# Clustered attention with a gated convolution on one core: two row moves become one transfer, an earlier load of the convolution weights, and another order

## The chip, the cores and the metric

The kernel runs on one core of a Trainium2 chip. The metric is device time in microseconds (us) of one execution. The median of three executions of the kernel before is 464.64 us (461.85 to 464.67). The engines are TensorE (PE in the rows; its weight loads PEld), VectorE (DVE), ScalarE (ACT), GpSimd (POOL) and SyncE (SP), which here issues every transfer between memories.

## The reference

Four batches of eight heads, 768 positions, 64 channels a head; then a gated projection over the 512 channels of a batch.

```python
q_assign = argmax(q_n @ c_n, axis=-1); k_assign = argmax(k_n @ c_n, axis=-1)
mask = q_assign[:, :, :, None] == k_assign[:, :, None, :]
scores = where(mask, scale * q @ k.T, -1e9)
attn = exp(scores - max(scores)); attn = attn / (sum(attn) + 1e-9)
x = (attn @ v)                       # heads side by side: [B, S, 512]
gate = sigmoid(causal_conv5(x, conv_w))
out = (gate * (x @ w_val)) @ w_out
```

The mask depends on the argmax over 16 clusters, so q and k are split into a high and a low part and their products are added up, to keep more digits than one pass of the product gives.

## The kernel before

There are 32 heads, taken in pairs (16 pairs, `p` below); four pairs make a batch. For a head `h` the work is:

- **Operands.** `load_both` (L438) loads kT and qT into alternate partitions of one `raw` tile. `prep_hi` (XH) rounds it to the high part in `ops[h][0]`, on ScalarE or VectorE (L217 or L219), and `prep_lo` (XL) makes the low part on VectorE (L213). Then transfers within the core's memory (`move`, L451) deal the rows out: MA copies the odd rows of the high part (q's) to the even rows of operand 2, MB copies the same rows to the even rows of operand 3, MC copies q's low part to the odd rows of operand 2, and MD overwrites the odd rows of operand 0 with its even rows, so MD has to wait until MA and MB have read. MK (`prep_mask`, L588) puts the cluster rows into operands 1 and 3.
- **Products.** QK (L624, L629) makes a tile of 128 x 768 scores from the four operands; six tiles a head. EX (L652) is their exponential on ScalarE, AD (L213, tile `ad`) adds the six tiles of a head together on VectorE.
- **Sums and values.** When a pair's adds are done, LL (L695) sums over partitions on TensorE; AV (L769) multiplies the probabilities with v (tile `vt`). SX (L785) scales the result on VectorE, five PC0/PC steps (L219 or L217, L800) are the convolution, PX and PL split it into high and low parts.
- **Projections.** "val" (L844) is x times w_val, VO (L850) applies the gate, VH and VL split the result, "proj" (L875) is its product with w_out. TensorE has 3 products for each step of 128 channels of either.
- **Clusters.** SI (L502) takes the similarities of a pair with the centroids; AM, A1, A2, A3 and FM make the cluster rows from it.

Every engine takes its instructions in a fixed order. For most of the program that order is written out as the table `PLAN`: 630 operations of VectorE, 681 of TensorE and those of the others, each number one operation of the list `todo`, with V or A for the engine where both can do it. The start stands ahead of it in code, and there the order is that of the lines: `load_cen`, `load_first`, `load_head(1, ...)`, `load_conv` (the convolution weights, 20 KB, tile `cbuf`), `load_v(0)`, `load_both(2)` and `load_both(3)`. CW (`prep_conv`) decodes these weights on VectorE with eight small instructions; PC of pair 0 needs them.

Of the kernel before, what the change touches and what calls it, by code (L numbers as in the profile page):

```python
# [8 lines left out]
F32 = mybir.dt.float32  # L9
# [8 lines left out]
P = 128  # L18
# [136 lines left out]
def kernel(  # L155
# [266 lines left out]
    raws, vs, ops, cleared = {}, {}, {}, {}  # L422
# [548 lines left out]
    for h in range(2, NH):  # L971
        if h < 4:
            LT = held("raw")
        else:
            LT = dma("LT", load_both, h, take="raw", after=[LT])
        LTS[h] = LT
        war = [last_qk[h - 2]] if h > 2 else []
        XH = Op("XH", "AV", prep_hi, h, after=[LT] + war)
        XL = Op("XL", "V", prep_lo, h, after=[XH]).frees(LT)
        z = [ZM[h]] if h in ZM else []  # L980
        MA = dma("MA", move, h, 2, 0, 0, 1, after=[XH])
        MB = dma("MB", move, h, 3, 0, 0, 1, after=[XH] + z)
# [3 lines left out]
        low[h], ready[h] = [MC, *z], [XL, MA, MB, MC, MD]  # L986

# [80 lines left out]
    for b in range(B):  # L1068
# [54 lines left out]
        591V 583 576 0 594 799.0 577 1 801A 800A 578 589A 579 2.0 580 581 587V 585A 3 1492 1415 w10.2 802.2 588A 4.1  # L1123
        603 610 6 586A 7.2 1416A 592 w11.0 9 12 10 11.3 803 13.4 582 584A 804 997.0 998 15 999 16.5 805 1417 1418
        1001A 1000A 593 806 14.0 5.1 1419 17 814.2 18 19.6 21 807.0 808 1420 596 815 1421 816 22.7 1002.1 1003.3 809
        1404 24 25.8 27 1422 28.9 29 8 1004 595 810 811 30 982 33 20 31.10 597A 34.11 599 590A 598 1005 1006 817 1007
        600 36 39 1008 1405A 37 601 1009 38.0 32 813 818 23 40.3 1423A 42 602 819.0 1406 45 1010 43.12 46.13 35 812
        1424 820 48 49.14 51 52.15 26 1014.2 1407 1408 1015 617 1425 624 54 1437 1409 41.0 604A 55 56.1 57 58.4 605
        1011 44 1410 47 1012 60 821 63 1016 61.2 64.5 1022.0 606 608 1017 1023 50 59.1 607 823 1024 1025A 826.2 1438A
        66 1018 1026A 822 827 69 611A 53 609 1019 612 614 613 67.6 70.9 615 1013 1027.0 1028.2 1029 1411 631 638 62 72  # L1130
        75 73 1412A 825 616 1439 65 1030 828 74.7 1031 1020 1021 78 68 824 1413 71 829 76.10 81 79.8 82.11 1414 1032
        983 830 84 85.0 87 1039.1 838.3 88.1 90 1040 831.1 1440 1041 618A 77.0 832 93 1033 1441 91 619 1442 1047.1
        1042 621 620 92.3 1048 94.4 622 96 99 833 97.2 100.12 95.1 1034 102 103.5 80 1443 1043 835 83 1049 98 1426 834
        105 623 839 1044 1035 1050A 625A 1051A 628 101 627 1493A 626 629 1036 837 1037 1038 86 1444 1052.1 106.13 108
        109 1427A 1495A 645 630 110.6 111 112.14 840 1053.3 1054 114 104 836 1445A 117 115.9 1045 1046 107 118.15 89
        841 1501A 1428 1055 120 121.3 984 1446 1429 123 124.7 1064.0 1065 126 652 1496 842 632A 1066 635 127 1430
        128.4 633 634 129 1056 1057 1497 636 1447 130.10 1067 843.2 844 1498 845 637 131.0 132 133.2 135 1072.0 1073
        136.8 1068 1499 850.2 1431 138 141 851 1494 847 134 639A 1058 1074 1059 846 1432 1060 1061 1062 1076A 139.11
        1503A 1069 142.12 1075A 849 642 659 641 113.1 144 147 145 146.0 148.5 116 1063 137 640 1077.0 150 153 1433 985
        1078.2 1079 1070 1080 1081 852 119 1082 140 154.1 122 151.13 643 143 1434A 1083 125 1504 1435 156 666 157.4  # L1140
        644 159 853 1436 1089.1 160.6 848 162 163 1090 1071 165 1505 854 1084 1085 646A 1091 649 1448 164.10 1097.1
        166.14 1098 648 168 1092 171 862.3 1500 169.2 172.9 1099 1506 647 1093 174 177 1100A 855.1 650 1101A 1094 651
        1449A 856 1502 1507 857 149.0 863 858 1450 167.1 152 1451 653A 656 864 1509A 1086 1087 1088 1102.1 1103.3 1104
        1105 986 654 859 1106 1107 1452 865 155 861 1510 1096 657 178.8 1108 1109 1095 655 175.15 1110 1508 170 673
        680 1525A 1111 1517A 1112 1113 658 180 1533.2 183 866 867.0 181 173 1518 1511A 860 182.3 1534 176 184.11 158
        186 187.7 189 179 868 1535 161 192 190.12 1536 193.0 195 198 1453 869 660A 1537 1454 1114.0 196.10 662 199
        874.2 663 661 1115 1455 664 875 200.5 871 1526 201 202.14 1456A 1586.0 185.0 1457 204 1116 876 207 205.13
        208.1 1122.2 1123 1124 1126A 203.1 877 1519A 1587 1588 1589 1590 210 211.2 213 1579.2 665 214.9 667A 1117 1580
        1512 870 216 1118 1458 1125A 219 1540.0 1541 1542 217 1581 220.15 218.4 668 1513 1514 222 669 1515 206 223.8
        1543 1544 225 226.6 1459 1582 1583 1527A 1460A 188 1119 1121 1461 228 670 1520 231 1127.0 1128.2 1462 873 1129  # L1150
        1463 674A 1464 1130 1131 1132 1133 229.3 987 687 878 1516 677 1134 1135 1465 1466 671 872 675 1136 1137 1138
        1467A 232.5 879.3 1468 1120 1469 1593.1 672 678 880 881 191 676 209 1470 194 212 234 237 235 236.11 1594 215
        197 883 694 1595 1596 1547.3 1548 240 1549 1471A 238.14 882 1597 1472 1139.1 241.7 1473 1140 243 244.13 1550
        1474 1475 1476 1147.1 679 1141 1477 1478A 1148 1551 246 247.12 1479 1480 1149 1481 249 1554.1 250.1 681A 1528
        252 253 254.0 683 1600.3 1142 1601 1602 1150A 255 256.2 258 1521 1603 684 261 1529 1522 1555 1530 1531 1556
        1557 682 1523 1151A 259.9 1482A 262.10 1143 1524 1483 885 1484 1485 1558 1532 1604 1625A 1486 1487 1488 264
        267 688A 1152.1 1489A 1153.3 1154 1155 1156 685 1157 1144 239.0 1490 988 1491 1146 1158 265.11 1159 691 1145
        1538A 884 1559V 686 1545A 886.2 1539 268.14 1560 1552A 221.1 270 1553 273 1546 701 708 271 272.4 224 1567.0
        887 888 274.15 689 1568 1569 1570 1172.2 1571 276 1173 227 277.8 279 1573.0 280.6 1174 692 889 890 690 693
        1633A 1572 1574 1575 891.2 242 230 892 282 1576 893 1176A 1175A 1561.2 1562 1563 1564 285 1577 283.7 245 248  # L1160
        1565 286.13 251 898.0 233 1584V 1585 1164.2 1626 895 894 288 291 1627A 715 899 1578 1165 695A 1605A 1160 1566
        1628 1166 1629 697 1161 897 289 698 290.3 1162 292.12 1630 1167 1163 294 1598A 297 1631 1632 696 1177.0 1178.2
        1179 1180 1181 1182 1183 1184 275.0 257.1 260 278 263 281 284 1168 1185 1186 1187 1188 298.1 266 989 295.5 300
        303 699 1169 1171 1170 722 269 287 910.3 301.4 702A 304.0 900 1189.1 901 902 1591A 896 700 306 309 911 704 307
        1592 703 1190 1191 706 1599 1606 903.1 1635V 1636 1192 308.2 310.15 1607.3 1608 904 905 311.0 705 312 315 1609
        1610 313.8 907 906 316.9 1634 318 321 1611 322.10 1619.1 1620 912 913 1197.3 1198 319.6 1637 314 1199 1621
        1622 707 324 325 327 914 1193 709A 710 1638 1639 1201A 326.7 328.11 1613.3 1614 1200A 317 330 909 320 333 1194
        1195 1651V 711 1615 1612 712 1623 293.1 915.1 331.14 334.13 1616 1649V 336 339 323 916 1650 296 716A 1624
# [173 lines left out]
```

## Time and profile before

| what | value |
|---|---|
| median of 3 executions | 464.64 us (461.85 to 464.67) |
| profiled execution | 463.09 us |
| its span, first to last instruction | 461.4 us |
| TensorE busy | 448.8 us (97%) |
| VectorE busy | 409.6 us (89%) |
| ScalarE busy | 296.0 us (64%) |
| GpSimd busy | 7.5 us (2%) |
| mean granted TensorE clock | 0.997 of full speed |
| transfers, mean | 137 GB/s |

The profiled execution is 1.55 us under the median and 1.69 us longer than its span. A busy share counts an instruction from its start to its end; TensorE's products overlap, so that its busy time is no measure of its work: the distance from one start to the next is. The chain of waits goes back from the last instruction, at each step to what released it.

### The profile page before, as it was taken

The page shows a single profiled execution, that of the slowest core. Times are in us where ns is not written, and L with a number is a line of the kernel's source. Part 1 is how long each engine was busy: PE and PEld are TensorE (multiplying, and loading weights), DVE is VectorE, ACT ScalarE, POOL GpSimd, SP SyncE. Part 2 cuts the span into 40 slices and gives each one's busy share as a digit, 9 for nine tenths or more (in the row PEclk, how much of TensorE's full clock was granted, in tenths as well). Part 3 has the DMA queues.
Part 4 walks back from the last instruction along what each step waited for, and adds up shares of the span by engine and source line. Part 5 has one row for each costly group of instructions (what it writes and reads, how often), then busy time and mean ns, then how long its engine had stood idle before and what let it go on. Part 6 is the DMA issues. An engine that isn't in the chain of part 4 may idle for free.

```text
span 461.4 us, 7538 instructions
## 1 busy us (share of the span) xinstructions
PE 448.8 (97%) x2633; PEld 320.1 (69%) x2633; DVE 409.6 (89%) x725; ACT 296.0 (64%) x437; POOL 7.5 (2%) x47
## 2 busy tenths in 40 slices
PE   7899999999999999999999999999999999999995
PEld 5556555654794968558597784948677696848984
DVE  4999999999999999999999998989998788796950
ACT  6988789867885787738584664768854465613131
POOL 5000000000000000000000000000000000001000
PEclk9999999999999999999999999999999999999998
DMA  7546656446446453544543156335542313200112
GB/s 213 196 141 209 203 167 223 169 139 200 143 131 198 146 185 123 167 119 138 172 150 133 53 186 213 102 131 170 184 160 83 105 46 100 82 0 25 45 38 105
DMA packets 32775, 63.38 MB, mean 137 GB/s; under 512 B 10588, under 2 KB 12764, under 8 KB 32732
## 3 DMA queue, kind: packets, MB, share of 16 engines
q1 hardware_dynamic: 32732, 62.85, 42.1%
q8 instruction: 22, 0.36, 0.3%
q14 instruction: 21, 0.17, 0.1%
HBM read 29.81 MB, written 6.38 MB: 78 GB/s over the span
## 4 chain that ended last, share of the span: by engine, by line
PE 72%; DVE 12%; DMA 8%; ACT 3%; SPq 2%; issue 2%; DVEq 0%; ACTq 0%
PE acc L769 20%; PE sp L624 12%; PE acc L875 11%; PE acc L844 11%; PE sp L629 10%; DVE ad L213 4%; DMA op<-op 2%; PE acc L695 2%; PE sp L844 2%; PE sp L875 2%; DVE gate L800 2%; PE acc L502 2%; ACT pt L652 1%; SPq L588 1%; DVE op L213 1%
## 5 line engine op out<-in xcount | busy, mean ns | idle before, releaser
L652 ACT ACTIVATE pt<-sp,sp 128x768 f32<-128x768 f32 x192 | 166.2, 898 | 58.6 <-PE sp L629 26.8
L769 PE MATMUL acc<-pt,vt 128*64 128x384 f32 x768 | 131.1, 490 | 0.6 <-ACT vt L217 0.6
L213 DVE TENSOR_TENSOR ad<-ad,pt 128x768 f32<-128x768 f32 x128 | 119.4, 951 | 2.0
L624 PE MATMUL sp<-op,op 128*128 128x384 f32 x372 | 101.9, 355 | 3.3 <-ACT pt L652 1.7
L769 PEld LDWEIGHTS acc<-pt,vt 128*64 128x64 f32 x768 | 52.2, 137 | 67.9 <-issue 61.7
L629 PE MATMUL sp<-op,op 128*128 128x384 f32 (+1 forms) x372 | 95.5, 337 | 0.0
L624 PEld LDWEIGHTS sp<-op,op 128*128 128x128 f32 x372 | 62.7, 188 | 30.0 <-ACT pt L652 15.8
L800 DVE SCALAR_TENSOR_TENSOR gate<-xr,cw,gate 128x768 f32<-128x768 f32 (+1 forms) x84 | 68.5, 823 | 0.9
L629 PEld LDWEIGHTS sp<-op,op 128*128 128x128 f32 (+1 forms) x372 | 67.4, 188 | 0.0
L875 PE MATMUL acc<-wh_o,h 128*128 128x512 f32 x144 | 51.3, 399 | 0.0
L844 PE MATMUL acc<-xh,wh_v 128*128 128x384 f32 x112 | 38.6, 344 | 0.0
L844 PE MATMUL acc<-xh,wl_v 128*128 128x384 f32 x112 | 37.8, 337 | 0.0
L844 PE MATMUL acc<-xl,wh_v 128*128 128x384 f32 x112 | 37.7, 337 | 0.0
L875 PEld LDWEIGHTS acc<-wh_o,h 128*128 128x128 f32 x144 | 27.1, 188 | 5.7 <-issue 0.6
L213 DVE TENSOR_TENSOR ad<-pt,pt 128x768 f32<-128x768 f32 x32 | 30.2, 948 | 0.8 <-ACT pt L652 0.8
L213 DVE TENSOR_TENSOR op<-raw,op 128x768 fp32r<-128x768 f32 (+2 forms) x34 | 30.4, 902 | 0.1
L875 PE MATMUL acc<-wl_o,h 128*128 128x512 f32 x72 | 28.6, 397 | 0.0
L881 ACT ACTIVATE ob<-acc 128x512 f32<-128x512 f32 (+1 forms) x22 | 12.5, 575 | 19.6 <-PE acc L875 16.5
L850 DVE SCALAR_TENSOR_TENSOR gate<-gate,acc 128x384 f32<-128x384 f32 x28 | 15.1, 549 | 8.5 <-PE acc L844 7.6
L217 ACT ACTIVATE op<-raw 128x768 fp32r<-128x768 f32 x24 | 20.2, 840 | 1.8 <-PE sp L624 1.8
L844 PEld LDWEIGHTS acc<-xh,wh_v 128*128 128x128 f32 x112 | 21.1, 188 | 0.2
L844 PEld LDWEIGHTS acc<-xh,wl_v 128*128 128x128 f32 x112 | 21.1, 188 | 0.2
(174 smaller groups left out, 483.8 us busy)
## 6 DMA issues: line engine op xcount, KB each, us to landing
op<-op SPq DMA_DIRECT2D x120, 192.0 KB, 2.3
raw<-kT SPq DMA_DIRECT2D x32, 192.0 KB, 3.7
raw<-qT SPq DMA_DIRECT2D x32, 192.0 KB, 3.3
vt<-v SPq DMA_DIRECT2D x16, 384.0 KB, 3.5
out_dram<-ob SPq DMA_DIRECT2D x23, 256.0 KB, 2.8
rs<-rr SPq DMA_DIRECT2D x30, 192.0 KB, 3.3
op<-oht SPq DMA_DIRECT2D x120, 24.0 KB, 1.9
h<-w_out SPq DMA_DIRECT2D x4, 512.0 KB, 3.9
```

What stands on the lines that cost most here:

```text
L213: (V if on[0] == "V" else G).tensor_tensor(out_, a, b, op=op)
L217: S.activation(out_, in_, AF.Copy, scale=x)
L502: PE.matmul(acc[32 * e:32 * e + 32, 0:HALF], (cen2[:, h % HB] if g else cenT[:, 0]).rearrange("p h c -> p (h c)"), raws[h][:, hf * HALF:(h ...
L624: PE.matmul(sp[:, hf, 0:HALF], x1[:, ts_], y1[:, hf * HALF:(hf + 1) * HALF], start=True, stop=False)
L629: PE.matmul(sp[:, hf, 0:HALF], x2[0:KR, ts_], y2[0:KR, hf * HALF:(hf + 1) * HALF], start=False, stop=True)
L652: S.activation(o.rearrange("p (a b) -> p a b", a=2), sp[:, :, 0:HALF], AF.Exp, bias=shift[h], scale=QS)
L769: PE.matmul(acc[e * D:(e + 1) * D, 0:HALF], vt[:, j, e * D:(e + 1) * D], pts[2 * p + e, j][:, hf * HALF:(hf + 1) * HALF], start=(j == 0), ...
L800: V.scalar_tensor_tensor(g, xr[:, k + c0:k + c1], cw[:, ct, k:k + 1], g, op0=ALU.mult, op1=ALU.add)
L844: PE.matmul(macc["v", b, ch, m][:, 0:HALF], a[:, kt, ms], x[:, kt, cs], start=(kt == 0 and i == 0), stop=(kt == NC - 1 and i == 2))
L850: V.scalar_tensor_tensor(gv, gv, 1.0, macc.pop(("v", b, ch, m))[:, 0:HALF], op0=ALU.add, op1=ALU.mult)
L875: PE.matmul(macc[b, ch, t, c0][:, 0:c1 - c0], x[kt][:, ts_], a[:, kt, c0:c1], start=(kt == 0 and i == 0), stop=(kt == NC - 1 and i == 2))
L881: S.activation(ob[:, 0:c1 - c0], acc[:, 0:c1 - c0], AF.Copy)
```

## The change

Operands 2 and 3 of a head from 2 on become two halves of one tile `mv`, and MA and MB become one transfer M2 whose source is read twice, so that it writes both halves. Before, MD waited for MA and MB; now it waits for M2. `load_conv` stands ahead of the two `load_head(1, ...)`. `PLAN` is another table. The engines' work is the same but for a few conversions that go to the other of ScalarE and VectorE.

```diff
-    raws, vs, ops, cleared = {}, {}, {}, {}
+    raws, vs, ops, moved = {}, {}, {}, {}
...
+    def move_both(h):
+
+        src = ops[h][0][1:P:2].bitcast(F32).unsqueeze(1).broadcast_to([D, 2, SQ])
+        nc.sync.dma_start(out=moved[h % 2][0:P:2].bitcast(F32), in_=src)
...
-        if i == 3 and h > 1:
-            if h % 2 not in cleared:
-                cleared[h % 2] = op_p.tile([P, SQ], F32R, name=f"op3_{h % 2}", bufs=1)
-            return cleared[h % 2]
+        if i > 1:
+            if h % 2 not in moved:
+                moved[h % 2] = op_p.tile([P, 2, SQ], F32R, name=f"mv_{h % 2}", bufs=1)
+            return moved[h % 2][:, i - 2]
...
-        MA = dma("MA", move, h, 2, 0, 0, 1, after=[XH])
-        MB = dma("MB", move, h, 3, 0, 0, 1, after=[XH] + z)
+        MA = dma("M2", move_both, h, after=[XH] + z)
         MC = dma("MC", move, h, 2, 1, 1, 1, after=[XL])
-        MD = dma("MD", move, h, 0, 1, 0, 0, after=[XL, MA, MB])
+        MD = dma("MD", move, h, 0, 1, 0, 0, after=[XL, MA])
...
     PLAN = """
-        591V 583 576 0 594 799.0 577 1 801A 800A 578 589A 579 2.0 580 581 587V 585A 3 1492 1415 w10.2 802.2 588A 4.1
...
+        769.0 577 0 3 1385 952 591V 576 583 770A 771A 581 1 580 579 589A w10.2 772.2 2.0 6 578 4.1 587A 588A 593 582
...
+    load_conv()
     load_head(1, "q")
     load_head(1, "k")
-    load_conv()
     load_v(0)
```

**First place: TensorE, ahead of LL of pair 10** (heads 20 and 21; `ad` are the two sums that VectorE's adds have made). Before:

```order
L875 MATMUL acc_3162<-wh_o,h_2856 128x512
L875 MATMUL acc_3162<-wl_o,h_2856 128x512
L875 MATMUL acc_3162<-wh_o,h_2856 128x512 x2
L875 MATMUL acc_3162<-wl_o,h_2856 128x512
L875 MATMUL acc_3162<-wh_o,h_2856 128x512 x2
L875 MATMUL acc_3162<-wl_o,h_2856 128x512
L875 MATMUL acc_3162<-wh_o,h_2856 128x512 x2
L875 MATMUL acc_3162<-wl_o,h_2856 128x512
L875 MATMUL acc_3162<-wh_o,h_2856 128x512
L502 MATMUL acc_3186<-raw_3124,cen_123 32x384 x2
L502 MATMUL acc_3186<-raw_3128,cen_123 32x384 x2
L695 MATMUL acc_3193<-ad_3036,wt_3065 32x384
```

Now (line numbers are 5 higher):

```order
L880 MATMUL acc_3040<-wh_o,h_2872 128x512
L880 MATMUL acc_3040<-wl_o,h_2872 128x512
L880 MATMUL acc_3040<-wh_o,h_2872 128x512 x2
L880 MATMUL acc_3040<-wl_o,h_2872 128x512
L880 MATMUL acc_3040<-wh_o,h_2872 128x512
L629 MATMUL sp_3101<-mv_232,op_0_2862 128x384 x2
L634 MATMUL sp_3101<-mv_232,op_0_2863 128x384 x2
L507 MATMUL acc_3106<-raw_2813,cen_123 32x384 x2
L507 MATMUL acc_3106<-raw_2824,cen_123 32x384 x2
L700 MATMUL acc_3117<-ad_2988,wt_2969 32x384
```

A whole "proj" of one 128-row block (12 products) and one "val" (12 products) that stood ahead of this LL now stand behind it; of every other kind TensorE has as many ahead of it as before. In VectorE's order the last add of head 20, on which this LL waits, is the 398th of the 630 planned operations in both. Ahead of it the new order has one PC0 of 768 columns, one SX, one VH of 384 columns and one step of the weights' decoding more, and one PX of 384 columns, one VO, one VS (v times its weight) and one XH less.

**Second place: SyncE, the transfers of head 20** (`op_0` is operand 0, `mv` operands 2 and 3). Before, MB, MA, MC and MD with what stands between:

```order
L451 DMA op_0_232<-op_0_2626 64x768
L482 DMA vt_2664<-v 128x768
L451 DMA op_1_2553<-op_1_2553 64x768
L451 DMA op_0_2628<-op_0_2626 64x768
L451 DMA op_0_2628<-op_0_2627 64x768
L588 DMA op_0_232<-oht 16x384 x2
L451 DMA op_0_2626<-op_0_2626 64x768
L588 DMA op_0_2627<-oht 16x384 x2
```

Now:

```order
L451 DMA mv_232<-op_0_2585 64x768
L593 DMA mv_232<-oht 16x384 x2
L456 DMA mv_232<-op_0_2584 64x2x768
L593 DMA op_0_2585<-oht 16x384 x2
L711 DMA lsum<-lr_2680 128x1x12
L451 DMA op_0_2584<-op_0_2584 64x768
```

M2 takes the place of the first and the fourth row; it comes after MC and one MK, and MD stands three issues behind it. Between M2's place in the plan and the first QK of head 20 TensorE has four QK tiles, four "val" steps and one small product.

**Third place: SyncE, the start.** Before:

```order
L493 DMA pt_155<-qT 128x768
L430 DMA raw_157<-kT 64x768 x2
L430 DMA raw_160<-qT 64x768 x2
L347 DMA cbuf<-conv_w 128x40
L482 DMA vt_164<-v 128x768
```

Now:

```order
L498 DMA pt_155<-qT 128x768
L347 DMA cbuf<-conv_w 128x40
L430 DMA raw_158<-kT 64x768 x2
L430 DMA raw_161<-qT 64x768 x2
L487 DMA vt_164<-v 128x768
```

One small load has moved ahead of four others of head 1. The instructions that decode it, which stood early in VectorE's order, come after the scores of head 2.

## Rows read from the trace of the kernel before

**Rows 1.** Windows of the span: length, then each engine's busy time (instructions), clock, transfers.

```profile
24.00:276.20 252.20, 250.14 (x1445) 171.66 (x1445) 244.93 (x421) 185.03 (x268) 0.00 (x0) 1.00 0.49 159
276.20:461.40 185.20, 179.97 (x1034) 135.18 (x1032) 147.48 (x257) 91.78 (x137) 1.47 (x2) 0.99 0.30 99
```

**Rows 2.** Longest waits of VectorE between 24 and 277: waiter, releaser: total, times, longest.

```profile
DVE nm L643 <- PE sp L629: 1.0, 3, 0.4
...
DVE ad L213 <- ACT pt L652: 0.4, 1, 0.4
```

**Rows 3.** Timeline around LL of pair 10: start, length, engine, line, operation, count.

```profile
273.37 2.81 DVE L213 TENSOR_TENSOR ad<-ad,pt 128x768 f32<-128x768 f32 x3
...
277.18 0.85 PE L502 MATMUL acc<-raw,cen 128*32 128x384 f32 x8
...
277.85 0.83 PE L695 MATMUL acc<-ad,wt 128*32 128x384 f32 x8
```

**Rows 4.** Chain of waits, pieces of back-to-back products: start, length, count.

```profile
378.14 6.31 PE acc L875 x27
...
429.43 4.24 PE acc L844 x24
```

**Rows 5.** VectorE by form: count, then busy time, mean ns of one, idle before.

```profile
L785 DVE TENSOR_TENSOR xr<-acc,rs 128x384 f32<-128x384 f32 x30 | 16.0, 548 | 1.0 <-DMA rs<-rr 1.0
L850 DVE SCALAR_TENSOR_TENSOR gate<-gate,acc 128x384 f32<-128x384 f32 x28 | 15.1, 549 | 8.5 <-PE acc L844 7.6 <-ACT gate L805 0.9
...
L219 DVE TENSOR_SCALAR h<-gate 128x384 fp32r<-128x384 f32 x12 | 4.3, 356 | 0.8 <-PE acc L875 0.6
...
L219 DVE TENSOR_SCALAR op<-raw 128x768 fp32r<-128x768 f32 x7 | 3.9, 556 | 0.6 <-DMA raw<-qT 0.3 <-PE sp L624 0.3
...
L219 DVE TENSOR_SCALAR vt<-vt,wt 128x384 f32<-128x384 f32 x7 | 2.8, 414 | 0.0
...
L366 DVE TENSOR_SCALAR h<-h 128x512 int32<-128x512 int32 x6 | 2.5, 421 | 0.1
...
L219 DVE TENSOR_SCALAR xh<-xr 128x384 fp32r<-128x384 f32 x6 | 2.1, 356 | 0.1
...
L219 DVE TENSOR_SCALAR gate<-xr,cw 128x768 f32<-128x768 f32 x2 | 1.2, 617 | 0.0
```

**Rows 6.** The page's transfers: issuer, count, size, median us from issue to landing.

```profile
op<-op SPq DMA_DIRECT2D x120, 192.0 KB, 2.3
raw<-kT SPq DMA_DIRECT2D x32, 192.0 KB, 3.7
raw<-qT SPq DMA_DIRECT2D x32, 192.0 KB, 3.3
vt<-v SPq DMA_DIRECT2D x16, 384.0 KB, 3.5
```

**Rows 7.** The moves' issue on SyncE, line 451: duration ns min/median/max.

```profile
L451 SPq DMA_DIRECT2D op<-op x120: 464/535/1791, 13.3 to 385.8; - x120
```

**Rows 8.** The page's chain of waits: shares of the span by engine, then by line.

```profile
PE 72%; DVE 12%; DMA 8%; ACT 3%; SPq 2%; issue 2%; DVEq 0%; ACTq 0%
PE acc L769 20%; PE sp L624 12%; PE acc L875 11%; PE acc L844 11%; PE sp L629 10%; DVE ad L213 4%; DMA op<-op 2%; PE acc L695 2%; PE sp L844 2%; PE sp L875 2%; DVE gate L800 2%; PE acc L502 2%; ACT pt L652 1%; SPq L588 1%; DVE op L213 1%
```

**Rows 9.** Waits of TensorE in the whole span: waiter, releaser: total, times, longest.

```profile
PE sp L624 <- DMA op<-op: 0.8, 2, 0.7
```

**Rows 10.** Timeline of the start, SyncE and VectorE.

```profile
2.31 1.20 SPq L430 DMA_DIRECT2D raw<-kT  x2
...
4.82 0.59 SPq L347 DMA_DIRECT2D cbuf<-conv_w  x1
...
12.66 0.56 DVE L219 TENSOR_SCALAR op<-raw 128x768 fp32r<-128x768 f32 x1 [0.35 <-DMA raw<-qT]
...
16.64 0.18 DVE L363 TENSOR_SCALAR cbuf<-cbuf 128x20 int32<-128x20 int32 x1
...
17.99 0.18 DVE L419 TENSOR_TENSOR cw<-cbuf 128x20 f32<-128x20 f32 x1
```

More of the change, by code (lines that the diff above doesn't have):

```diff
@@ L980 @@
         z = [ZM[h]] if h in ZM else []
-        MA = dma("MA", move, h, 2, 0, 0, 1, after=[XH])
-        MB = dma("MB", move, h, 3, 0, 0, 1, after=[XH] + z)
+        MA = dma("M2", move_both, h, after=[XH] + z)
         MC = dma("MC", move, h, 2, 1, 1, 1, after=[XL])
-        MD = dma("MD", move, h, 0, 1, 0, 0, after=[XL, MA, MB])
+        MD = dma("MD", move, h, 0, 1, 0, 0, after=[XL, MA])
         XHS[h] = XH
-        low[h], ready[h] = [MC, *z], [XL, MA, MB, MC, MD]
+        low[h], ready[h] = [MC, *z], [XL, MA, MC, MD]
     C2 = Op("C2", "P", spread_cen, None, take="acc")
@@ L1128 @@
[L1128 to L1132, printed above, removed]
@@ L1213 @@
[L1213 to L1215 removed]
+        769.0 577 0 3 1385 952 591V 576 583 770A 771A 581 1 580 579 589A w10.2 772.2 2.0 6 578 4.1 587A 588A 593 582
+        773 601 585V w11.0 9 7.2 774 1386V 586A 775 607 10 776 592 12 584A 1387 613 11.3 777.0 967.2 968 13.4 15 14.0
@@ new lines @@
+        1050 1051 1052 1053 1405 1054 1055 1471A 160.0 140 157.7 955 1406 638A 1040 1472 143 1056 825.0 826 827 125
+        162 163 165 1041 640 1475 832.0 164.6 1418 166.13 1059.3 833 1060 829 168 169.2 1476 1061 1067.0 1068 171
+        172.3 639 1057 1477 174 149.0 641 661 1069 1062 1070A 1071A 1419A 177 644A 1420 178.8 167.1 1058 1072.3 645
+        642 152 834 1421 1470 1073.0 1074 175.9 1422 170 1423 1063 1479A 1075 1076 1077 1078 828 835 646 647 1079 180
+        183 155 181 1064 182.4 1481A 836 1080 1081 667 184.11 1424 173 1065 1487A 1082 1083 186 189 158 831 187.10 830
@@ new lines @@
+        848 1433 1096A 203.1 226.8 849.1 228 843 231 679 1434 1486 1521 850 1435 206 1436 194 1437A 1438 1439 1097.1
+        1098.2 1090 662A 1099 209 1100 1101 663 842 1102 1103 229.4 232.5 851 1091 1104 1105 1106 1107 1108 212 197
+        1440 1441A 664 665 234 666 856.3 215 235 852 1109.0 236.11 1442 237 857 1443 1110 1111 240 1444 1117.3 1445
+        1446 1447 238.13 1490 241.10 1563.0 243 246 853 1448A 1564 244.12 1498 1112 1449 1565 1450 247.14 1113 249
+        250.2 252 1118 1566 1451 1114 253 1499 239.0 254.1 668A 1567 669 671 255 1524.3 1525 670 256.15 258 1526 259.6
@@ new lines @@
+        315 1160 313.6 1589.2 876 316.9 881 1167.1 318 321 319.12 293.0 311.1 1168 322.0 692A 1611A 1583.1 882 883
+        1161 884 1162 1169 324 1613A 325 326.3 1606 327 1584 1585 1590 328.13 1171V 1591 330 1163 1164 709 333 693
+        331.11 695 1592 334.8 1170A 1586 1607 1593 1608 336 1587 694 878 879 339 698A 314 1609 1610 317 1166 1614
+        885.2 296 886 1172.1 1173.0 299 1174 1175 1176 1177 340.7 1178 1594 1179 1180 1181 1182 696 699 337.14 1183
+        715 1615 342 960 345 320 302 305 701 323 1616 343 887 1165 344.4 1629V 1619V 889 1184.2 892.3 1620 329.0
@@ new lines @@
+        1883V 1870 1766 574.12 572 1838 1351 575 1839V 1871 1352 1840 1353 1877A 1354 1355 1356 1357 1363 1358 1367
+        1878 1879 1880 1359.0 1853.3 1854 1855 1856 1360 1361.2 1868 1914.0 1362 1886 1907.1 1881 1847.1 1915 1848
+        1849 1371 1364 1368 1921.2 1372.0 1365.2 1366 1891V 1800 1812 1857 1875A 1928.3 1369.3 1850 1887 1373 1876
+        1841.2 1842 1843 1844 1953.0 1954 1929 1370 1858 1908 1901A 1888 1902 1903 1899A 1892 1851 1872 1873 1909 1884
+        1916 1917 1852 1955 1910 1893A 1900 1889 1890 1967.3 1968 1969 1874 1956 1922 1923 1845 1846 1957 1894 1911
@@ L1216 @@
+        1924 1958V 1918 1919A 1959 1974.1 1882 1912V 1960.2 1961 1962 1975 1904 1905 1976 1913 1963 1920 1941.1 1942
+        1981.0 1925 1926A 1927 1943 1935.0 1964 1895 1896 1897 1965V 1906 1977 1970 1966 1930 1898 1931 1932 1933V
+        1934 1971 1982 1999.2 2000 1947.2 1944 1948 1949 1950 1945 1946 1972V 1978 1973 1979A 1980 2001 1951 1952
+        1993.3 2002 1983 1936 1937 2003 2004 1984 1985 1986 1938 1939 1987.1 1940 1988 1989 1990 1991 1992 1994 1995
+        1996 1997 1998
     """
```

152 lines of the change are left out of this document (65 added, 87 removed).

## The prediction

> **What bounds the kernel now.** I read the windows first, to see which engine is full in which part of the span; then the chain of waits, to see whether a transfer or an engine carries the end; then the timeline at the one place where the change moves TensorE's work across a wait on VectorE; then the durations.
>
> In the windows [rows 1] the reader is to see two parts. Up to 276.2 us VectorE is busy 244.93 of 252.2 us, so it has 7.3 us of idle time there, and of these only some 3.8 us, five lines, have another engine or a transfer behind them [rows 2]; the rest are the small steps between instructions. After 276.2 VectorE has 147.48 us of work in 185.2, and TensorE is the engine that always has something. So the first part is set by how much work stands in VectorE's list, and the second by how much TensorE still has to do when VectorE lets it go on. The granted clock is 1.00 and 0.99 in the two [rows 1], the upper of the two levels; it plays no part. The chain of waits agrees [rows 8]: 72% TensorE, 12% VectorE, 8% transfers, 2% SyncE's queue; the moves of operands (op<-op) hold 2% of it, 9.2 us of 461.4.
>
> From this the end can be worked out at any place where TensorE waits for VectorE: the time when VectorE is there, plus what TensorE has left. A new order changes the total of neither engine, but it can change how much TensorE has left at such a place.
>
> **The new order.** The place I take is LL of pair 10, which waits for the last add of head 20. In the kernel before the three adds that end with it start at 273.37 and take 2.81 us [rows 3], so the sum is ready at 276.18. TensorE starts this LL at 277.85 [rows 3], after the similarities of a pair at 277.18, so it came 1.7 us after VectorE had been ready. There VectorE did not hold it up.
>
> In the new order VectorE's work up to that add is the same: 398 operations in both. The exchange is 617 + 548 + 356 + 421 ns more (PC0, SX, VH, a decoding step) and 356 + 549 + 414 + 556 ns less (PX, VO, VS, XH) [rows 5], 0.1 us net, which I drop. But TensorE has two groups of twelve products that stood ahead of this LL behind it now. A "proj" product of 512 columns takes 6.31 / 27 = 0.234 us in a run without a wait, a "val" product of 384 columns 4.24 / 24 = 0.177 us [rows 4]. That is 12 x 0.234 + 12 x 0.177 = 2.8 + 2.1 = 4.9 us. TensorE would arrive 4.9 us earlier. The 1.7 us by which it came late before take up that much, and for the rest it has to wait for VectorE: 4.9 - 1.7 = 3.2 us, by which everything behind this LL ends later. Nothing hides it: VectorE has no work to leave out before, and after it TensorE is the full engine. Queued behind the waiting LL are the twelve AV steps of pair 10, for which SX of that pair waits.
>
> What could take from the 3.2 us is idle time of VectorE ahead of the place: at most the 3.8 us of waits that have a releaser [rows 2], if the new order removes all of them (3.2 - 3.8 = -0.6). If it has twice as many, it is 7.0. I take 3.2, since the new order changes neither the operations ahead of that add nor their number, and keep -0.6 and 7.0 for the range.
>
> **One transfer for two moves.** It removes 30 issues of 0.535 us [rows 7], 16 us of SyncE's queue. How long M2 takes is not in the trace. A move of 192 KB lands after 2.3 us; loads of 192 KB land after 3.3 and 3.7 us and one of 384 KB after 3.5 [rows 6]. So the size alone adds between -0.2 and 0.2 us, which gives 2.1 to 2.5 us; the other end is twice a move, 4.6 us. I take 2.4, by the loads, which are the nearest rows in which only the size of one issue changes. The pair of before was over 0.5 + 2.3 = 2.8 us after MA's issue at the earliest. MD could then go some 0.4 us earlier, and behind it QK of the head. I cost this at nothing: TensorE's waits for such a move are 0.8 us in the whole span, in two places [rows 9], and the first part is VectorE's anyway. The ends are -9.2 us (all that the moves hold in the chain) and the slower case below.
>
> The Trainium skill, page "DMA: Bandwidth & Descriptors", section "Anatomy of one DMA", has a fixed cost of about 2.0 us and adds the bytes over 436 GB/s; by it I estimate 2.9 us for M2 and 2.45 for one move. The trace's 2.3 is a little under that for the single move. By that rule M2 lands about when the pair did, and the slower case below would not come about.
>
> **The convolution weights.** Their load moves ahead of four loads of head 1, which are issued 0.59 us later [rows 10]. VectorE's first wait on a load ends at 12.66 with a load of head 2 [rows 10], and that one keeps its place. So 0 is taken, between 0 and 0.6. The decoding, 16.64 to 18.17 [rows 10], 1.5 us, comes later in VectorE's list, and is ahead of the place above in both orders: 0. If PC of pair 0 waited for it, VectorE would have other work in its list in between.
>
> **Sum.** Against the profiled execution: 463.1 + 3.2 + 0 + 0 = 466.3 us. That execution stands 1.5 us under the median of the three, so the forecast is 0.4% above the median of 464.64. Within 1% of the median, about what a measurement of this kernel can tell from no change, is 460.0 to 469.3. The forecast's own range, from -0.6 and 7.0 us, is 462.5 to 470.1.
>
> **Rivals.**
>
> *The moves were what held the first part.* For it: the chain passes through op<-op and through SyncE's issues, 2% each [rows 8], and a transfer whose wait sits in a queue delays every later one in it; M2 takes one of the four moves of each head off that queue. Against: 0.8 us of TensorE's waits are for them [rows 9], and VectorE is busy 97% of the first part. If half of the 9.2 us of the chain goes and the order costs nothing, it is 463.1 - 4.6 = 458.5 us, faster.
>
> *M2 becomes the gate.* MD cannot start until M2 has landed whole, and QK of the head waits for MD. It happens where M2 stands close ahead of its head's first QK. At head 20 TensorE has four QK tiles of four products and twelve "val" products in between, 28 x 0.177 = 5.0 us [rows 4]. An M2 of 4.6, an issue of 0.5 and an MD of 2.3 us need 7.4, so QK comes 2.4 us late. Counted in the same way, heads 3, 6, 7 and 14 have 6.1, 6.1, 5.4 and 7.0 us: 1.3 + 1.3 + 2.0 + 0.4 us more. Together 7.4 us, 463.1 + 7.4 = 470.5 us, slower, without the 3.2 of the order. With M2 at 2.4 only head 20 is late, by 0.2 us; with the 3.2 us of the order added, the mechanism decides from an M2 of about 3.6 us on. For it: one transfer that writes two rows for each row of its source has no row here. Against: the loads, where twice the size costs 0.2 us [rows 6].
>
> *The new order costs nothing.* The 24 products behind LL fill waits that TensorE has later, or VectorE arrives earlier by its 3.8 us [rows 2]. Then it stays at 463.1 us. Against: TensorE is the full engine after 276.2 and has few waits to fill.
>
> **Chances and range.** The forecast gets 0.46, the order that costs nothing 0.12, the relieved moves 0.21, the gate 0.21. The predicted time is that of the first, 466.3. Faster by over 1% (under 460.0) is the second rival's kind alone, the relieved moves, with a little for an order that helps more than I can see: 0.22. Slower by over 1% (over 469.3) is the gate and the top of the forecast's own range: 0.22. Within 1%: 0.56. For 8 in 10 the range goes from 457.5, a little below the relieved moves, to 471.0, a little above the gate.
>
> **What would show it.** In the profile after, the lines of VectorE in the first 276 us should be as full as now, and the add of head 20 should end at 275 to 277 us. LL of pair 10 should start within 0.5 us of that add, with VectorE named as what ended TensorE's wait, where now TensorE comes 1.7 us later; the remaining time from this LL to the end should be near 183.5 + 4.9 = 188.4 us (now 461.4 - 277.85 = 183.5). M2 should land after 2.1 to 2.9 us, and TensorE's waits for moves stay under 2 us. SyncE should have 30 issues less. I am wrong in the main step if the add of head 20 ends clearly earlier than 275 us: then the first part was not VectorE's work alone; wrong in the size if LL starts later than the add again; and the gate is there if M2 lands after more than 3.6 us and QK of heads 20 and 7 waits for MD.

## The result, and the profile after

The changed kernel takes 459.49 us (median of 8 runs, 458.43 to 460.52) against 464.44 us for the kernel before beside it (8 runs, 461.85 to 467.0): ratio 0.9915, interval 0.9892 to 0.9938. By this ratio it is 0.85% faster, where 0.4% slower was forecast. The time lies in the predicted range; the direction is wrong. Ratios, here and below, leave out executions over 1.5% above the fastest of their kernel; that concerns three of the load alone (468.0 to 468.9 us).

The windows of the changed kernel, divided at the end of the last add of head 20 (270.1 us, where it was 276.2 in [rows 1]):

```profile
24.00:270.10 246.10, 245.82 (x1433) 168.75 (x1435) 242.70 (x427) 183.24 (x270) 0.00 (x0) 1.00 0.50 163
270.10:457.80 187.70, 183.44 (x1053) 138.82 (x1045) 147.58 (x257) 90.30 (x137) 1.52 (x2) 1.00 0.28 95
```

Three things are to be seen against [rows 1]. VectorE's idle time in the first part fell from 7.27 to 246.10 - 242.70 = 3.40 us. TensorE's fell too, from 252.20 - 250.14 = 2.06 to 0.28 us. And the second part is longer, 187.7 us, as more work stands in it. The granted clock is 1.00 in both, and in the kernel before, where [rows 1] has 0.99, it falls only after the last product; so the clock is no part of the difference between the two profiled spans.

VectorE's waits between 24 and 271, all of them, where [rows 2] had five lines with 3.8 us:

```profile
DVE st L517 <- PE acc L507: 0.2, 1, 0.2
DVE nm L648 <- PE sp L634: 0.2, 1, 0.2
```

The timeline of the changed kernel around LL of pair 10 (now L700), first TensorE, then VectorE; it answers to [rows 3]:

```profile
269.01 0.51 PE L629 MATMUL sp<-mv,op 128*128 128x384 f32 x2
269.36 0.51 PE L634 MATMUL sp<-mv,op 128*128 128x384 f32 x2
269.80 0.85 PE L507 MATMUL acc<-raw,cen 128*32 128x384 f32 x8
270.46 0.83 PE L700 MATMUL acc<-ad,wt 128*32 128x384 f32 x8
...
268.26 1.82 DVE L213 TENSOR_TENSOR ad<-ad,pt 128x768 f32<-128x768 f32 x2
```

The add ends at 268.26 + 1.82 = 270.1 and LL starts at 270.46, 0.4 us later. No row ahead of LL has a wait: TensorE goes from the QK products to the similarities and to LL, each start within 0.7 us of the one before. So both engines reach this place at nearly the same moment, and neither stands there. LL came 7.4 us earlier than before (277.85), and from it to the end it is 457.8 - 270.5 = 187.3 us instead of 183.5.

The page's transfers, where [rows 6] had op<-op x120:

```profile
mv<-op SPq DMA_DIRECT2D x30, 384.0 KB
...
mv<-op SPq DMA_DIRECT2D x30, 192.0 KB
op<-op SPq DMA_DIRECT2D x30, 192.0 KB
```

These are M2, MC and MD, 90 in place of 120.

**Where the 3.6 us of the two profiled spans lie.** A ruler that serves all runs: the time of LL of a pair, less all the work that TensorE has ahead of it, each operation of the order at one fixed duration (a QK tile 0.66 us, an AV step 0.66, LL and SI 0.65, a val step 0.52, a proj step 0.70, the small products less, from the trace of before). The level means little, but a difference between two runs is time that TensorE did not work or worked slower. By stages, in us, worked out from the trace of each run ("old" and "new" are the two orders):

| run | up to LL 0 | LL 0 to 5 | LL 5 to 10 | LL 10 to 15 | LL 15 to the end | span |
|---|---|---|---|---|---|---|
| before: old, two moves | 17.6 | 13.0 | 5.6 | 4.8 | 7.1 | 461.4 |
| old, two moves, new conv load | 16.8 | 13.6 | 5.6 | 5.0 | 7.2 | 461.4 |
| old, M2 | 16.5 | 12.2 | 5.6 | 4.2 | 7.4 | 459.3 |
| new, two moves, old conv load | 17.0 | 11.7 | 5.4 | 5.0 | 6.1 | 458.5 |
| new, two moves | 16.8 | 11.8 | 5.3 | 5.0 | 6.2 | 458.4 |
| after: new, M2 | 18.0 | 10.4 | 5.3 | 4.7 | 6.1 | 457.8 |

The second row is the order and the moves of before once more, so it shows what another execution makes of them: 0.6 us more from LL 0 to LL 5, at most 0.2 behind. Against before, the changed kernel gained 2.6 us between LL 0 and LL 5 (38 to 155 us) and 1.0 after LL 15; nothing much at LL 10, the place of the prediction. The stage up to LL 0 differs by up to 1.5 us between these executions and is not read.

Now the stage from LL 0 to LL 5 as one window, TensorE's busy time first after the length, VectorE's third. The kernel before:

```profile
38.00:155.00 117.00, 114.94 (x679) 74.47 (x680) 114.45 (x201) 91.13 (x130) 0.00 (x0) 1.00 0.56 181
```

The same order and moves in another execution (the load alone):

```profile
38.00:155.00 117.00, 114.32 (x677) 73.74 (x676) 114.01 (x199) 90.98 (x130) 0.00 (x0) 1.00 0.57 181
```

M2 in the old order:

```profile
38.00:155.00 117.00, 115.69 (x682) 74.84 (x683) 114.67 (x200) 91.43 (x132) 0.00 (x0) 1.00 0.56 181
```

The new order with two moves:

```profile
38.00:155.00 117.00, 116.45 (x684) 75.33 (x685) 114.79 (x202) 89.87 (x130) 0.00 (x0) 1.00 0.55 174
```

The changed kernel:

```profile
38.00:155.00 117.00, 117.00 (x698) 75.48 (x691) 116.03 (x205) 91.41 (x132) 0.00 (x0) 1.00 0.54 174
```

TensorE's idle time goes 2.06, 2.68, 1.31, 0.55, 0.00 us, and VectorE's column is highest where it is 0.00. The 1.31 is not M2's doing: two later runs with M2 and the old order in this window have 2.01 and 2.53. In the kernel before these are TensorE's waits in that window, by name; in the changed kernel there is none:

```profile
PE sp L624 <- DMA op<-op: 0.7, 1, 0.7
PE acc L769 <- ACT vt L217: 0.6, 1, 0.6
PE sp L624 <- ACT lr L702: 0.6, 1, 0.6
PE sp L624 <- issue: 0.2, 1, 0.2
```

One is for a move, two are for ScalarE, and they are short. In the load alone they are three, all for ScalarE, 2.6 us. In this stage the gain of the change is that such waits are gone: 2.06 of the 2.6 us.

The 1.0 us after LL 15 has another place. TensorE has no named wait there in either kernel, but ScalarE has one, ahead of its last copy from the accumulators. The last copy in the kernel before and in the changed one:

```profile
457.31 0.38 ACT L881 ACTIVATE ob<-acc 128x256 f32<-128x256 f32 x1 [0.97 <-DMA out_dram<-ob]
...
453.62 0.38 ACT L886 ACTIVATE ob<-acc 128x256 f32<-128x256 f32 x1 [0.47 <-PEq L1304]
```

Before, this copy waits until an earlier store has left its buffer `ob`, of which there are two; in the changed kernel it only waits for its product. From the start of the last product to the end of the span the kernel before takes 5.3 us and the changed one 4.5: 0.8 of the 1.0 us. All sixteen traces of this document are of one kind or the other. The twelve whose program ends in the old order have this wait for the store, 0.7 to 1.8 us, and 5.0 to 6.6 us from the last product's start to the end; the four that end in the new order have no such wait, and 4.5 to 4.7 us.

### The profile page after: what moved, and what is told of

It is laid out like the page before. It is cut to its first block, busy times and chain, and to the rows that moved or that the text cites. A ratio compares the mean times of both kernels' runs of the same rounds, so it can differ in the third digit from the quotient of the medians.

```text
span 457.8 us, 7516 instructions
## 1 busy us (share of the span) xinstructions
PE 447.9 (98%) x2633; PEld 321.1 (70%) x2633; DVE 407.5 (89%) x725; ACT 292.6 (64%) x437; POOL 7.6 (2%) x47
## 5 line engine op out<-in xcount | busy, mean ns | idle before, releaser
L629 PE MATMUL sp<-mv,op 128*128 128x384 f32 x372 | 101.7, 354 | 0.9 <-ACT pt L657 0.9
L634 PE MATMUL sp<-mv,op 128*128 128x384 f32 (+1 forms) x372 | 95.6, 337 | 0.0
L629 PEld LDWEIGHTS sp<-mv,op 128*128 128x128 f32 x372 | 63.4, 188 | 25.4 <-ACT pt L657 13.8
L634 PEld LDWEIGHTS sp<-mv,op 128*128 128x128 f32 (+1 forms) x372 | 67.4, 188 | 0.3 <-issue 0.3
L880 PE MATMUL acc<-wh_o,h 128*128 128x512 f32 x144 | 50.3, 397 | 0.0
L213 DVE TENSOR_TENSOR op<-raw,op 128x768 fp32r<-128x768 f32 (+1 forms) x32 | 29.5, 924 | 0.1
L849 PEld LDWEIGHTS acc<-xl,wh_v 128*128 128x128 f32 x112 | 21.0, 188 | 0.0
```

The lines of the kernel that those rows point to most:

```text
L213: (V if on[0] == "V" else G).tensor_tensor(out_, a, b, op=op)
L629: PE.matmul(sp[:, hf, 0:HALF], x1[:, ts_], y1[:, hf * HALF:(hf + 1) * HALF], start=True, stop=False)
L634: PE.matmul(sp[:, hf, 0:HALF], x2[0:KR, ts_], y2[0:KR, hf * HALF:(hf + 1) * HALF], start=False, stop=True)
L849: PE.matmul(macc["v", b, ch, m][:, 0:HALF], a[:, kt, ms], x[:, kt, cs], start=(kt == 0 and i == 0), stop=(kt == NC - 1 and i == 2))
L880: PE.matmul(macc[b, ch, t, c0][:, 0:c1 - c0], x[kt][:, ts_], a[:, kt, c0:c1], start=(kt == 0 and i == 0), stop=(kt == NC - 1 and i == 2))
```

## The experiments

**Which part of the change carries it.** Four kernels: the new order without M2 and with the old place of the convolution load; M2 with the order of before; the load alone; and the new order and load with two moves.

The first and the last are the changed kernel with this edit, the first also with `load_conv()` back behind the two `load_head`:

```diff
     def move_both(h):
...
-        src = ops[h][0][1:P:2].bitcast(F32).unsqueeze(1).broadcast_to([D, 2, SQ])
-        nc.sync.dma_start(out=moved[h % 2][0:P:2].bitcast(F32), in_=src)
+        move(h, 2, 0, 0, 1)
+        move(h, 3, 0, 0, 1)
```

The second is the changed kernel with `load_conv()` back and `PLAN` of before in the new numbers (first lines shown), the third is the kernel before with the load moved:

```diff
     PLAN = """
-        769.0 577 0 3 1385 952 591V 576 583 770A 771A 581 1 580 579 589A w10.2 772.2 2.0 6 578 4.1 587A 588A 593 582
...
+        591V 583 576 0 593 769.0 577 1 771A 770A 578 589A 579 2.0 580 581 587V 585A 3 1462 1385 w10.2 772.2 588A 4.1
```

```diff
+    load_conv()
     load_head(1, "q")
     load_head(1, "k")
-    load_conv()
```

> The new order alone: MA and MB stay two transfers, issued one behind the other at M2's place, and the convolution weights load at their old place. If the order is the cause (VectorE waits less for others in its first 276 us: 0.7 us of waits over 0.05 us in the place of 4.3), it is 459 to 460.5 us, as the whole change. If the transfer M2 is the cause (fewer issues, MD earlier), it is 463 to 465 us, as the kernel before.

Measured: 460.31 us (459.49 to 461.42) against 463.3, ratio 0.9937, interval 0.9913 to 0.996.

> The order of before with M2 in the place of MA and MB (at the earlier of the two places, for head 3 behind the clearing of its tile), weights loaded at the old place. If the order is the cause: 463 to 465.5 us, no change. If the transfer is the cause: 459 to 461 us.

Measured: 462.69 us (460.62 to 464.76), ratio 0.9989, 0.9965 to 1.0013. From the page of this run:

```profile
mv<-op SPq DMA_DIRECT2D x30, 384.0 KB, 2.9
...
op<-op SPq DMA_DIRECT2D x30, 192.0 KB, 2.2
mv<-op SPq DMA_DIRECT2D x30, 192.0 KB, 2.8
```

> The kernel before with only the load of the convolution weights ahead of head 1's loads. All theories: 463.5 to 465.5 us, no change; if the start carried a part of the gain, 1 us less or more, with VectorE's first conversion of head 2 at another time than 12.66.

Measured: 464.05 us (460.73 to 468.86), ratio 1.0007, 0.9976 to 1.0039.

> The changed kernel with M2 made two transfers of half the size again, all else as changed. If M2 is worth nothing in the new order: 459 to 460.5 us. If fewer issues carry the gain: 462 us or more. If M2 in one piece is a gate that costs something: under 459 us.

Measured: 460.35 us (460.06 to 460.85), ratio 0.9935, 0.9912 to 0.9958.

So the order carries 0.63 to 0.65% of the 0.85%, and for the load nothing is seen (0.9976 to 1.0039). M2 alone can't be told from nothing; on top of the new order it takes the ratio from 0.9935 to 0.9915, and those intervals overlap. From LL 0 to LL 5 the stage table gives it 0.8 us in the old order, but three later runs with M2 and the old order there have 12.7, 13.3 and 13.5, against 13.0 and 13.6 without M2, so that is not more than executions differ by. In the new order it gives 1.3 to 1.4, and a later run has this too (10.5 beside 10.4, against 11.7 and 11.8). M2 lands after 2.9 us and a single move into `mv` after 2.8 in the M2-alone run; these are medians of the 5 and 11 of 30 transfers whose landing the trace has, and the trace of the changed kernel has none.

**Which engine sets the end.** Work is taken off VectorE or TensorE in the kernel before, early or late, alone or both. The early edits are below; the late ones have the pairs (4, 5, 6) and (6, 7, 8, 9).

```diff
     def av(p, hf, j):
+        if j in (2, 3) and p in (1, 2, 3, 4):
+            return
...
     def post_conv(p, k, c0, c1):
+        if k > 1 and p in (0, 1, 2):
+            return
```

> The kernel before, with nine of VectorE's convolution steps (the third to fifth of pairs 0, 1 and 2, about 75 to 125 us) left out, so the gate of these pairs is not the reference's. Nine steps of 768 columns take 9 x 0.85 = 7.6 us from start to start. Theory A, the one of the prediction (VectorE sets the end up to 276 us): 5 to 7.6 us faster, and the last add of head 20 as much earlier. Theory B (VectorE sets it only up to about 150 us, from then on TensorE is the full engine): 2.5 to 6 us faster here too, LL of pair 5 earlier by as much.

Measured: 462.89 us against 463.62, ratio 1.0, 0.997 to 1.003. By the trace the nine steps are more than the 7.6 us of the text: the instructions of VectorE up to the last add of head 20 sum up to 280.5 us, 8.9 less than before. That add ends 2.2 us earlier, at 274.0, but from LL of pair 10 to the end it is 1.5 us longer than before, 1.3 of it at the wait for the store at the end. So in this execution VectorE's relief is seen at that add, and lost behind it.

> The kernel before, with nine of VectorE's convolution steps (the third to fifth of pairs 4, 5 and 6, about 175 to 245 us) left out, so the gate of these pairs is not the reference's; 7.6 us of VectorE's work as in the early case. Theory A (VectorE sets the end up to 276 us): 5 to 7.6 us faster, as in the early case. Theory B (from about 150 us on TensorE is the full engine): 0 to 1.5 us faster; the last add of head 20 ends earlier, and LL of pair 10 starts long after it.

Measured: 463.41 us, ratio 1.0, 0.9975 to 1.0025. Both theories fall on the early case, and the prediction's on both: 8.9 us off VectorE are worth nothing that can be told. In the late case, the window 165 to 276, before and in this run:

```profile
165.00:276.00 111.00, 111.00 (x638) 79.75 (x637) 107.33 (x179) 72.51 (x108) 0.00 (x0) 1.00 0.44 143
165.00:276.00 111.00, 111.00 (x638) 80.14 (x637) 99.41 (x171) 72.61 (x108) 0.00 (x0) 1.00 0.44 143
```

And VectorE's longest wait there:

```profile
DVE nm L643 <- PE sp L629: 6.2, 4, 3.4
```

TensorE is busy all 111 us in both. VectorE, 7.92 us less busy than before, waits 6.2 us for QK, and the last add of head 20 ends at 275.9, only 0.3 us earlier.

> The kernel before, without two of the six AV steps of pairs 1 to 4 (about 45 to 125 us), so x of these pairs is not the reference's: 32 products of 0.157 us from start to start, 5.0 us of TensorE's work. Theory A (VectorE sets the end up to 276 us): 0 to 1 us faster, TensorE only waits longer. Theory B (VectorE up to about 150 us, then TensorE): 0 to 1.5 us faster.

Measured: 461.25 us, ratio 0.9949, 0.9921 to 0.9977. The last add of head 20 ends at 273.3, 2.9 us earlier.

> The kernel before, without two of the six AV steps of pairs 6 to 9 (about 175 to 260 us), so x of these pairs is not the reference's: 32 products, 5.0 us of TensorE's work. Theory A (VectorE sets the end up to 276 us): 0 to 1.7 us faster, the 1.7 us being the time by which LL of pair 10 starts after the last add of head 20. Theory B (from about 150 us on TensorE is the full engine): 3.5 to 5 us faster.

Measured: 463.3 us, ratio 0.9995, 0.9979 to 1.0012. The amount in these two texts is too low: each of the 32 products is two rows of the trace (64 rows fewer here, 2569 for 2633), and 0.157 us is the mean step of one row, so about 10 us were taken off. Even so the late case gains nothing. The same window in this run (the profiled execution is its fastest, 460.93 us):

```profile
165.00:276.00 111.00, 103.93 (x577) 75.41 (x579) 107.22 (x179) 71.94 (x108) 0.00 (x0) 1.00 0.43 146
```

And TensorE's longest waits there:

```profile
PE acc L502 <- DVE xr L787: 3.6, 3, 1.9
PE acc L695 <- DVE ad L213: 3.0, 3, 1.3
```

Now TensorE waits for VectorE, 3.0 us of it in LL for the adds, and VectorE is as busy as in before (107.22 for 107.33). The last add of head 20 ends at 274.7, 1.5 us earlier. Theory B, which had TensorE alone as the full engine from 150 us on, falls with this; and the 2.4 us of the early AV case are more than either theory allowed.

> The kernel before, without the nine convolution steps of pairs 4 to 6 and without two of the six AV steps of pairs 6 to 9, both cuts of the two late cases together (so the gate and x of these pairs are not the reference's): 7.6 us less on VectorE and 5.0 us less on TensorE between about 175 and 260 us. Theory C (both engines are full at the same time there, and each holds the end alone once the other is relieved): 4 to 5 us faster, though neither cut alone gave more than 0.3. Theory D (neither engine sets the end there, a chain of short waits does): the sum of the two alone, 0 to 0.6 us faster.

Measured: 458.06 us against 463.28, ratio 0.9866, 0.9835 to 0.9898: 5.2 us, where either alone gave 0.0 and 0.05%. The last add of head 20 ends at 271.4, 4.8 us earlier, where either alone made it 0.3 and 1.5.

> The kernel before, without the nine convolution steps of pairs 0 to 2 and without two of the six AV steps of pairs 1 to 4, both early cuts together (so the gate and x of these pairs are not the reference's): 7.6 us less on VectorE and 5.0 us less on TensorE between about 45 and 125 us. Alone they gave 0 and 2.4 us. Theory C (both engines are full there too): 4 to 5 us faster. If TensorE alone sets the end there: 2 to 3 us faster, as with the AV steps alone. If VectorE alone does: the 0 of the convolution steps alone.

Measured: 459.5 us against 463.44, ratio 0.9909, 0.9873 to 0.9945: 3.9 us by the medians, where either alone gave 0.0 and 0.5%. (Here and in the late case about 10 us are again taken off TensorE.) In the late stretch the two engines are full at once, theory C: this is shown outright. In the early stretch it is not shown. The interval of both together overlaps that of the AV steps alone, and the last add of head 20 ends 3.8 us earlier (272.4) where either alone made it 2.2 and 2.9, so that the two together give less than their sum.

**Where in the order the gain is.** The changed kernel with one of the two orders up to LL of pair 6 and the other behind it; what one part leaves for the other to do differs, so such a seam costs something itself. Some 25 operations that take a buffer get another of the same kind. The first row of `PLAN` that differs from the changed kernel, behind LL of pair 6 in the first kernel:

```diff
-        1541 1143 1555 1597V 1598 1561V 282 283.0 285 1599 1548 1542 868.0 1600 680A 1134.3 286.8 869 1135 1601 288
```

and at the very start in the second:

```diff
-        769.0 577 0 3 1385 952 591V 576 583 770A 771A 581 1 580 579 589A w10.2 772.2 2.0 6 578 4.1 587A 588A 593 582
+        591V 583 576 0 593 769.0 577 1 771A 770A 578 589A 579 2.0 580 581 587V 585A 3 1462 1385 w10.2 772.2 588A 4.1
```

> The changed kernel with its own order up to LL of pair 6 (about 185 us), and the order of before for all that is left. If the gain comes from the first part (as the times of LL say: LL of pair 5 came 4.5 us earlier with 2.3 us more left to do): 2 to 3 us faster than before. If it comes from the part around LL of pair 10, as the prediction had the effect of the order: 0 to 1 us faster.

Measured: 462.77 us, ratio 0.999, 0.9969 to 1.0012.

> The changed kernel with the order of before up to LL of pair 6 (about 187 us), and its own order for all that is left. If the gain comes from the first part: 0.5 to 1.5 us faster than before (the last 1.1 us come after LL of pair 15). If it comes from the part around LL of pair 10: 2.5 to 3.5 us faster.

Measured: 463.31 us, ratio 1.0002, 0.9977 to 1.0027.

By the times alone both expectations fail. By stages: new then old has 10.5 us from LL 0 to LL 5, as the changed kernel (10.4), then 7.6 to LL 10 (5.3 to 5.6 without a seam) and 7.5 at the end, as before. Old then new has 12.7, then 7.8, and 6.1 at the end, as the changed kernel. So each half shows the gain of its own part, and the seam, 2.2 us between LL 6 and LL 10 in either run, 1.3 to 1.8 of them right behind LL 6, eats it. The gain at the start is seen in the first run and that at the end in the second; that either is worth its full size alone is not shown by a time.

**The predicted wait by itself.** M2 with the order of before, and only the 24 products moved behind LL of pair 10, with the VectorE steps that need them, in two versions. In `PLAN` 1234 is this LL, 1669 to 1672 the proj and 1681 to 1684 the val; the rows of the second version:

```diff
-        718 1214 368 397 389 398.3 399 371 400.9 392 1221A 1669.1 1670 1671 402 403.1 1678 721 717 727 733 405 1632
...
+        1664 722A 719 1665 1666 395 374 377 1215 904.1 1234.0 1667 1669.3 1670 1671 1672 1673 1674 1681.3 1682 1683
```

> M2 with the order of before and the old place of the convolution load (the M2-alone case, 462.69), and of the new order only the one thing on which the prediction's main step rests: the twelve proj and twelve val products that stood ahead of LL of pair 10 stand right behind it; VO and VH of that val follow them, 0.9 us less ahead on VectorE. Prediction's step (VectorE is there at its old time less 0.9, LL waits for it, 4.9 us more stand behind): 2 to 3 us slower than the M2-alone case; LL of pair 10 within 0.5 us of the add, 1.5 to 3 us earlier than there, and 4.9 us more from it to the end. Rival (the products stood in VectorE's way as well, so that it comes as much earlier): 0 to 0.5 us slower, LL 4.4 to 4.9 us earlier.

Measured: 470.82 us against 463.28, ratio 1.0143, 1.0107 to 1.0178. VectorE stood 7.6 us at VO of the moved val, which its fixed order has behind the last add of head 20 and ahead of those of head 22, so this time can't tell the theories apart. LL of pair 10 starts at 277.8, 1.1 us after the add, and not earlier than with M2 alone (276.0).

> M2 with the order of before and the old place of the convolution load, and the twelve proj and twelve val products ahead of LL of pair 10 put behind it, as in the earlier case, but with VO, VH and VL of that val nine VectorE operations later, so that VectorE doesn't stand waiting for the moved products (it lost 7.6 us there in the earlier case). Prediction's step (VectorE is at the add at its old time, TensorE waits for it with its own work moved behind): 2 to 4.9 us slower than the M2-alone case of 462.69, LL of pair 10 where it was or up to 2.5 us earlier. Theory C says the same. Rival (the products were in VectorE's way): LL 4 to 5 us earlier, 0 to 0.5 us slower.

Measured: 468.82 us against 463.44, ratio 1.0114, 1.0079 to 1.0149; 6.1 us over M2 alone. The timeline on TensorE and VectorE:

```profile
268.51 0.61 PE L629 MATMUL sp<-mv,op 128*128 128x384 f32 x2 [1.41 <-ACT pt L657]
...
272.36 2.81 DVE L213 TENSOR_TENSOR ad<-ad,pt 128x768 f32<-128x768 f32 x3
...
275.55 0.85 PE L507 MATMUL acc<-raw,cen 128*32 128x384 f32 x8
276.22 0.83 PE L700 MATMUL acc<-ad,wt 128*32 128x384 f32 x8
276.98 0.50 PE L880 MATMUL acc<-wh_o,h 128*128 128x512 f32 x1
```

The add ends at 275.2 and LL starts at 276.2, where it was 274.3 and 276.0 with M2 alone. With 4.9 us less ahead of it LL came no earlier, as the prediction's step had it, and from LL to the end it is 7.9 us longer than with M2 alone in the profiled executions: the 4.9 and 3.0 more. But the wait is not the one that was predicted. LL goes 0.7 us after the similarities, which start after the add has ended, so it does not wait for the add. TensorE lost its time further ahead: two waits of QK for ScalarE's exponentials, 1.7 us, of which the first line shows the longer, and others before. So that moved products come back as waits is seen, and that LL waits for the add is not seen here; it is in the late AV case (3.0 us in three places).

## Why the prediction was wrong

**The step that failed** is "I take 3.2, since the new order changes neither the operations ahead of that add nor their number": VectorE at the add of head 20 at its old time. The operations are nearly the same, but it was there at 270.1, not 276.2; the prediction had named that as the sign that the first part is not VectorE's work alone. Summed over the trace, VectorE's 468 instructions up to this add take 289.4 us in both kernels, one by one. What changed lies between them: the gaps add up to 13.1 us before and 9.2 after, and the stretches in which an instruction starts before the last one ends to 27.3 and 29.5. That is 3.9 + 2.2 = 6.1 us.

The bound of 3.8 us for it, from the waits with a releaser [rows 2], was too small, since waits are only the larger half. Gaps of over 0.15 us fell from 14 with 8.7 us in all to 7 with 5.3: 3.4 us. The other 2.7 us are in no list of waits. Neighbours on VectorE either overlap, mostly by some 81 ns, or the second starts some 34 ns after the first has ended. Three instructions in a row of the kernel before show both:

```profile
232.09 0.36 DVE L643 TENSOR_REDUCE nm<-sp 128x1 f32<-128x192 f32 x1 [0.27 <-PE sp L629]
232.49 0.15 DVE L647 TENSOR_SCALAR sp<-nm 128x1 f32<-128x1 f32 x1
232.56 0.55 DVE L785 TENSOR_TENSOR xr<-acc,rs 128x384 f32<-128x384 f32 x1
```

The second reads what the first wrote and starts 0.04 us after its end; the third reads nothing of the second and starts 0.08 us before its end. So it is at all 23 row maxima and all 10 reciprocals of this stretch, and of the 110 gaps of up to 50 ns before, 102 lie between two instructions of which the second reads a tile that the first wrote. In the new order there are 93 such gaps, 17 fewer, 15 of them of this kind; at 34 + 81 ns each they make 2.0 us. So it counts which operations stand next to each other in VectorE's list, although these are nearly the same. This sum says where the 6.1 us lie; it does not say that VectorE alone could have used them, for with 8.9 us less to do in the late case it was at the add only 0.3 us earlier.

**Behind it** stands the reading of [rows 1]: "the first part is set by how much work stands in VectorE's list". VectorE is busy 97% there, but TensorE is busy 99%, and I left that out because overlapping products make its busy share look full anyway. The runs show both full at once in the late stretch: 8.9 us off VectorE or 10 us off TensorE gave nothing there, both together 5.2. For the early stretch, where most of the gain lies, that is argued only. There TensorE idles 2.06 us of 117.00 and VectorE 2.55, so a short wait of either has little room to be made up; a new order that adds no work can remove such waits, and did, 2.06 us on TensorE between 38 and 155 us. Why this order has none of them is open.

**What was right.** Products moved behind a wait lengthen what is left: 188.4 us from LL to the end were forecast, 187.3 measured, and with these products moved in the old order (VO, VH and VL of that val behind them) the kernel became 5.4 us slower. LL starts within 0.5 us of the add, though by TensorE's own arrival and not by a wait. M2 was taken at 2.4 us with 2.1 to 2.9 as the sign; it is 2.9 in the M2-alone run, and no gate: the changed kernel's trace names no wait of TensorE for a move between operands. By the Trainium skill, page "DMA: Bandwidth & Descriptors", section "Anatomy of one DMA — SWDGE (gpsimd) path", the estimate was 2.9; the section gives its fit for transfers that GpSimd issues, and these are SyncE's, but the 2.9 of the M2-alone run agrees with it. For a single move the same estimate was 2.45, and the runs have medians from 2.1 to 2.9. The convolution load at 0: ratio 1.0007. The prediction calls the wait that ends at 12.66 VectorE's first on a load; an earlier one, of 0.98 us, is for the centroids, which are loaded ahead of all that moved. 30 issues fewer: as said.

**The rivals.** "The new order costs nothing", with VectorE earlier by its 3.8 us, had VectorE's earlier arrival right and its size too small, at a chance of 0.12. "The moves were what held the first part" gave 458.5, close to the time, for the wrong reason: with two moves the new order is already at 0.9935, and what M2 adds, some 0.2%, could not be told from nothing.

**As a sum:** VectorE at the add 6.1 us earlier, TensorE's lateness at LL down from 1.7 to 0.4 us, so LL 7.4 earlier; 3.8 us more from there to the end; 3.6 us of span. The 3.8 is itself 4.9 of moved products less 1.0 gained after LL 15, 0.8 of it at ScalarE's last copy. That end of the program stands nowhere in the prediction: it took everything behind LL as TensorE's work.

## What to carry to other kernels

When two engines are each about 97% busy or more in a stretch, ask what relieving both is worth, not which is the bound: taking work from one alone may show nothing. An engine's arrival at a place is not its work plus a fixed idle time; a new order can take out the gaps and the lost overlap, and only the distance from start to start shows how much that is. Look at the last instructions of the program by themselves, whatever engine they are on: a wait of 0.97 us there was worth 0.8. A piece of an order tried alone may cost what the whole order gains, since the rest of it is made to fit.

## What was not expected of the hardware

A transfer that writes two rows for each row it reads, 384 KB in all, lands after 2.9 us; a move of 192 KB into the wide tile `mv` takes 2.8 and one into a plain operand 2.2 in the same run. That the two single moves differ does not come from the tile. In the run with the new order up to LL of pair 6 and the old one behind it, the move into `mv` takes 2.2 as well:

```profile
mv<-op SPq DMA_DIRECT2D x30, 384.0 KB, 2.9
mv<-op SPq DMA_DIRECT2D x30, 192.0 KB, 2.2
op<-op SPq DMA_DIRECT2D x30, 192.0 KB, 2.1
```

So twice the bytes and a second destination cost 0.7 us there. What else is under way when a move is issued may make the difference between 2.2 and 2.8; that was not tried. Each of these medians rests on 5 to 11 transfers of 30, and single ones take up to 5.3 us.

The other thing is VectorE's neighbours, which stood 34 ns apart where the second reads what the first wrote and mostly overlapped by some 81 ns otherwise: some 0.12 us for each such pair, where an instruction takes 0.15 to 1 us.
